# The two halves of the first q load are issued by one queue instead of two

## The chip, the core and the metric

The kernel runs on one core of a Trainium2 chip. The core has a matrix engine (TensorE, "PE" in the profile, with its weight loads as "PEld"), a vector engine (VectorE, "DVE"), a scalar engine (ScalarE, "ACT"), a general engine (GpSimd, "POOL") and a synchronisation engine (SyncE, "SP") that in this kernel does nothing but issue DMAs. DMAs are issued by SP, ACT and POOL, each into a queue of its own, and carried out by 16 DMA engines. The metric is the device time of one execution in microseconds, the median over several runs.

## What is computed

Attention over 8 batches, 12 heads, 448 positions and 64 values a head, with an RMS norm of q and k ahead of it, and behind it a dense layer with a tanh GELU and a second dense layer. Cut to what matters:

```python
q: (8, 12, 448, 64); k, v the same; g_q, g_k: (64,); moe_w_in: (768, 2048); moe_w_out: (2048, 768)

def rmsnorm(x, g):
    rms = np.sqrt(np.mean(x * x, axis=-1, keepdims=True) + 1e-06)
    return x / rms * g
q_n, k_n = rmsnorm(q, g_q), rmsnorm(k, g_k)
scores = (1 / 8) * np.matmul(q_n, k_n.transpose(0, 1, 3, 2))
attn = np.exp(scores - np.max(scores, axis=-1, keepdims=True))
attn = attn / (np.sum(attn, axis=-1, keepdims=True) + 1e-09)
x = np.matmul(attn, v)            # then to (3584, 768)
h = x @ moe_w_in
g = 0.5 * h * (1.0 + np.tanh(c * (h + 0.044715 * h * h * h)))   # c = sqrt(2 / pi)
out = g @ moe_w_out               # float32
```

## The kernel before

**Tiling.** A batch has three chunks of four heads. A chunk's q is one tile `raw` of 128 partitions by 2 x 7 x 64 floats (two heads side by side in the partitions, two more along the free side, called halves a = 0 and a = 1; seven positions to a partition), and its k another one. So a load of a chunk's q or k is 448 KB, and half a of it 224 KB. A unit (line 324) is one seventh of a chunk's keys against all queries: four matmuls into a PSUM tile and one exponential of 128 x 896 on ACT (line 337, `ex`). A batch is 21 units. Behind the units come the sums over keys and the products with v (line 384), their reciprocals and transposes on DVE, then the first dense layer (lines 422 and 473) with GELU, and the second dense layer (line 443), whose matmuls fill the gaps of the next batch's attention.

**Order.** The order on each engine is written by hand: what the program says first runs first on its engine. Each engine runs its own list in that order and waits by semaphores for what it needs. Tiles come from pools; a tile of a pool that is all in use waits until its old content has been read.

**The start**, which the change touches, is lines 613 to 723, before the first units:

- Line 614 makes the first q tile and the two loads of its halves; lines 616 to 623 add the loads of the first k in two pieces: positions 0 to 3 of each partition (`t_first`, 256 KB) and 4 to 6 (`t_rest`, 192 KB). Lines 624 and 625 issue all four. Half 0 of q is issued by SP, half 1 by ACT, both pieces of k by SP. `load` (line 115) issues part i on `engs[i]`.
- Line 626 loads the row g_k on ACT's queue (`load_g`, two pieces of 128 bytes, which land in a tile that POOL clears first, line 83); g_q came before on POOL's queue (line 91). Line 627 loads ACT's table for exponential and logarithm.
- Lines 628 and 629 issue, on SP, q and k of chunk 1 and of chunk 2 (448 KB each); lines 725 to 727 do the same for batch 1 beside the first units.
- Lines 678 to 682: ACT squares half 0 and half 1 of q (line 159), DVE sums each over 64 values (line 170); then the same for k's first piece. Lines 687 and 688 make the reciprocal roots on ACT (logarithm at line 195, exponentials at 202 and 214). Lines 690 to 692 scale q on POOL and DVE and k's first piece on DVE (line 273).
- Lines 694 to 696: POOL squares chunk 1's q and k (line 161, into a free part of the tile `g`), one square for q and two for the halves of k. DVE sums these at lines 721 to 723, behind its scaling of k's second piece at line 720. Then POOL goes on to v's loads (lines 697 and 698), chunk 2's squares (699 and 700) and the loads of the first weights (701).
- Lines 702 to 719: transposes of q and k by PE, copies to `qT` and `kT` by ACT and DVE (line 291, lines 300 to 304), and the bound `shift` for the exponentials.
- Then the units run (line 768). In the list of what goes between units, chunk 1's reciprocal roots (`rsqrt(0, 1)`) stand on ACT behind the third unit's exponential (line 734), and chunk 1's scaling on DVE behind them.

The few lines around the change:

```python
t_first, t_rest = slice(0, 4), slice(4, NT)
halves = load(0, 0, "q", 2, (nc.sync, nc.scalar))      # line 614
raws["k", 0, 0] = rawqk.tile([P, 2, NT, D], F32, tag="rawk", name="rawk")
halves += [lambda ts=ts: nc.sync.dma_start(...) for ts in (t_first, t_rest)]
for go in halves:
    go()
load_g(1, g_k, nc.scalar)
nc.scalar.preload_act_table_set(EXP_SET)
loads(0, 1)
loads(0, 2)
```

Of the kernel before, what the change touches and what calls it, by code (L numbers as in the profile page):

```python
# [17 lines left out]
def kernel(  # L18
# [11 lines left out]
    nc = tc.nc  # L30
# [84 lines left out]
    def load(b, c, n, parts=1, engs=(nc.sync,)):  # L115
        t = rawqk.tile([P, 2, NT, D], F32, tag=f"raw{n}", name=f"raw{n}")
        src = {"q": q, "k": k}[n]
        raws[n, b, c] = t
        m = 2 // parts
        return [  # L120
            lambda i=i: engs[i].dma_start(
                t[:, i * m:(i + 1) * m].rearrange("p a t d -> p a (t d)"),
                src[b, 4 * c + 2 * i * m:4 * c + 2 * (i + 1) * m].rearrange(
                    "(a r) (p t) d -> (r p) a (t d)", r=2, t=NT
                ),
            )
            for i in range(parts)
        ]
# [482 lines left out]


    t_first, t_rest = slice(0, 4), slice(4, NT)
    halves = load(0, 0, "q", 2, (nc.sync, nc.scalar))
    raws["k", 0, 0] = rawqk.tile([P, 2, NT, D], F32, tag="rawk", name="rawk")
    halves += [
        lambda ts=ts: nc.sync.dma_start(  # L617
# [278 lines left out]
```

## Time and profile before

| what | value |
|---|---|
| time, median of 3 runs | 405.6 us (405.19 to 406.0) |
| time of the profiled execution | 405.4 us |
| its span, first to last instruction | 403.6 us |
| TensorE clock that was granted | 0.999 |
| PE busy | 393.4 us, 97% of the span |
| ACT busy | 281.0 us, 70% |
| DVE busy | 257.7 us, 64% |
| POOL busy | 123.0 us, 30% |
| PE idle from the span's start to 10 us | 2.97 us |
| PE idle from 10 to 20 us | 2.59 us |
| PE idle from 20 to 30 us | 0.92 us |
| PE idle from 30 to 300 us | 0.0 us |

All times inside the profile are microseconds from the span's start. A line of the timeline has start, duration, engine, line of the program, operation, output<-inputs, shapes, count, and in brackets how long the engine sat idle before it and what ended that. A q behind an engine's name (SPq, ACTq) is its issuing part: a line with it is the issue of a DMA, not its transfer. The chain of waits is followed back from the last instruction, at each step to what released it; a DMA in it counts from its issue to its landing. A DMA lands when all the engines that carry it have reported.

### The profile page before, as it was taken

The page shows a single profiled execution, that of the slowest core. Times are in us where ns is not written, and L with a number is a line of the kernel's source. Part 1 is how long each engine was busy: PE and PEld are TensorE (multiplying, and loading weights), DVE is VectorE, ACT ScalarE, POOL GpSimd, SP SyncE. Part 2 cuts the span into 40 slices and gives each one's busy share as a digit, 9 for nine tenths or more (in the row PEclk, how much of TensorE's full clock was granted, in tenths as well). Part 3 has the DMA queues.
Part 4 walks back from the last instruction along what each step waited for, and adds up shares of the span by engine and source line. Part 5 has one row for each costly group of instructions (what it writes and reads, how often), then busy time and mean ns, then how long its engine had stood idle before and what let it go on. Part 6 is the DMA issues. An engine that isn't in the chain of part 4 may idle for free.

```text
span 403.6 us, 8096 instructions
## 1 busy us (share of the span) xinstructions
PE 393.4 (97%) x3321; PEld 209.8 (52%) x3321; DVE 257.7 (64%) x436; ACT 281.0 (70%) x382; POOL 123.0 (30%) x103
## 2 busy tenths in 40 slices
PE   7799999999999999999999999999999999999996
PEld 3365555555555555554555555555555545555564
DVE  5998858985796369845699357963698405990010
ACT  6995498868974887847975689748878359744301
POOL 4993407364007230093004540072301800000000
PEclk9999999999999999999999999999999999999999
DMA  8999995998515954169612938139413511110033
GB/s 280 312 212 208 200 211 210 239 233 228 97 41 105 256 97 143 41 162 288 107 41 63 255 60 221 40 85 275 69 41 80 115 24 39 50 47 24 2 78 80
DMA packets 65561, 54.07 MB, mean 134 GB/s; under 512 B 37364, under 2 KB 60532, under 8 KB 65524
## 3 DMA queue, kind: packets, MB, share of 16 engines
q1 hardware_dynamic: 53184, 41.48, 38.3%
q0 software_dynamic: 12112, 11.80, 18.8%
q8 instruction: 26, 0.43, 0.4%
q10 hardware_dynamic: 228, 0.28, 0.3%
q14 instruction: 11, 0.09, 0.1%
HBM read 45.61 MB, written 11.01 MB: 140 GB/s over the span
## 4 chain that ended last, share of the span: by engine, by line
PE 94%; ACT 2%; DMA 2%; POOL 1%; DVE 0%; SPq 0%; issue 0%
PE o L443 38%; PE h L422 24%; PE t L473 12%; PE t L333 9%; PE t L384 8%; ACT ex L337 2%; DMA rawq<-in_q_dram 2%; PE o L384 1%; POOL g L161 1%; PE tp L291 1%; SPq L617 0%; PE os L384 0%; DVE st L393 0%; DVE ss L170 0%; PE o L266 0%
## 5 line engine op out<-in xcount | busy, mean ns | idle before, releaser
L337 ACT ACTIVATE ex<-t,shift 128x896 bf16<-128x896 f32 x168 | 157.6, 1005 | 22.0 <-PE t L333 19.4
L443 PE MATMUL o<-wout,g 128*128 128x384 bf16 (+1 forms) x912 | 156.8, 324 | 0.0
L443 PEld LDWEIGHTS <-g 128*128 128x128 bf16 x912 | 83.6, 98 | 67.7 <-issue 18.8
L422 PE MATMUL h<-xT,win 128*128 128x448 bf16 x516 | 99.1, 352 | 0.0
L170 DVE TENSOR_REDUCE ss<-sq 128x14 f32<-128x896 f32 (+3 forms) x45 | 44.3, 999 | 49.1 <-ACT sq L159 46.1
L422 PEld LDWEIGHTS <-win 128*128 128x128 bf16 x516 | 50.5, 98 | 47.1
L428 ACT ACTIVATE g<-h 128x448 bf16<-128x448 f32 x86 | 46.6, 543 | 28.2 <-PE h L422 23.1
L453 DVE COPY osb<-o 128x384 f32<-128x384 f32 x41 | 22.7, 554 | 52.6 <-PE o L443 50.6
L333 PE MATMUL t<-qT,kT 64*64 64x448 bf16 x672 | 47.0, 359 | 3.0 <-DVE kT L300 1.0
L473 PE MATMUL t<-xT,win 128*128 128x448 bf16 x252 | 49.6, 352 | 0.0
L478 ACT ACTIVATE g<-t 128x896 bf16<-128x896 f32 x21 | 18.4, 915 | 33.0 <-PE t L473 33.0
L666 POOL COPY mark<-es 1x1 bf16<-1x1 bf16 x6 | 1.1, 177 | 131.5 <-DVE es L355 131.5
L273 POOL TENSOR_TENSOR nrmq<-rawq,rinv 128x896 bf16<-128x896 f32 (+1 forms) x21 | 34.8, 1658 | 12.0 <-DVE o L236 7.7
L473 PEld LDWEIGHTS <-win 128*128 128x128 bf16 x252 | 24.5, 98 | 22.8 <-issue 0.6
L273 POOL TENSOR_TENSOR nrmk<-rawk,rinv 128x896 bf16<-128x896 f32 x20 | 33.5, 1679 | 0.0
L333 PEld LDWEIGHTS <-kT 64*64 64x64 bf16 x672 | 17.4, 105 | 28.1 <-issue 20.8
L384 PE MATMUL t<-ex,vb 64*64 64x448 bf16 x588 | 31.6, 350 | 0.0
L451 ACT COPY osb<-o 128x384 f32<-128x384 f32 (+1 forms) x16 | 7.3, 458 | 31.5 <-PE o L443 31.5
L400 DVE STREAM_TRANSPOSE rb<-rc 128x896 f32<-128x896 f32 x24 | 26.7, 1111 | 0.8
L358 DVE TENSOR_TENSOR e<-ex 128x896 bf16<-128x896 bf16 x33 | 20.0, 607 | 9.7 <-ACT ex L337 9.4
L384 PEld LDWEIGHTS <-vb 64*64 64x64 bf16 x672 | 20.4, 107 | 11.1 <-issue 2.4
L393 DVE STREAM_TRANSPOSE st<-t 128x448 f32<-128x448 f32 x42 | 24.6, 625 | 1.0 <-PE t L384 0.9
(93 smaller groups left out, 294.5 us busy)
## 6 DMA issues: line engine op xcount, KB each, us to landing
out_dram<-osb SPq DMA_DIRECT2D x54, 192.0 KB, 2.7
rawq<-in_q_dram SPq DMA_DIRECT2D x23, 448.0 KB, 4.3
rawk<-in_k_dram SPq DMA_DIRECT2D x23, 448.0 KB, 5.5
vb<-in_v_dram POOLq DMA_DIRECT2D x7, 672.0 KB, 6.7
win<-in_moe_w_in_dram POOLq DMA_DIRECT2D x8, 384.0 KB, 11.0
wout<-in_moe_w_out_dram POOLq DMA_DIRECT2D x2, 1536.0 KB, 24.0
vb<-in_v_dram POOLq DMA_DIRECT2D x1, 448.0 KB, 10.5
qT<-nrmq SPq DMA_TRANSPOSE x19, 4.9
```

The costliest lines, as they stand in the source:

```text
L170: nc.vector.reduce_sum(sss[b][:, seat(b, c), "qk".index(n), hs, ts], squares(b, c, n, hs, ts), axis=AX.X)
L273: eng.tensor_mul(nrms[n, b, c][:, ts].rearrange("p t a d -> p a t d"), raws[n, b, c][:, :, ts], root[:, :, ts].to_broadcast([P, 2, m, D]),)
L333: nc.tensor.matmul(sc[r * R:(r + 1) * R, a, :S], kT[rs, c, t, r], qT[b][rs, c, :, r], start=True, stop=True,)
L337: nc.scalar.activation(ex[:, t], sc[:, :, :S], AF.Exp, scale=scale, bias=shift)
L384: nc.tensor.matmul(o[r][a * D:(a + 1) * D], vb[b % 2][rs, 2 * c + a, i] if what else ones[rs], es[i][rs, a], start=(i == 0), stop=(i == n ...
L393: nc.vector.transpose(st[:, r].rearrange("p a b -> p (a b)"), oas[0][r])
L400: nc.vector.transpose(rb.rearrange("p r s -> p (r s)"), rc.to_broadcast([128, 2 * S // 32, 32]))
L422: nc.tensor.matmul(h[:, :S], win[:, c, f * 128:(f + 1) * 128], xT[b][:, c], start=(c == 0), stop=(c == HP - 1),)
L428: nc.scalar.activation(g[:, f, (b % 2) * S:(b % 2 + 1) * S], h[:, :S], AF.Gelu_apprx_tanh)
L443: nc.tensor.matmul(o, g[:, f, i * 128:(i + 1) * 128], wout[:, f, lo:hi], start=(f == 0), stop=(f == nf - 1),)
L453: nc.vector.tensor_copy(osb[:, lo:hi], o)
L473: nc.tensor.matmul(h[:, j, :S], win[:, c, f * 128:(f + 1) * 128], xT[b][:, c], start=(c == 0), stop=(c == HP - 1),)
```

## The change

The second half of the first q (half 1, 224 KB) is issued by SP, not by ACT. SP's list then begins with half 0, half 1, k's first piece, k's second piece, and goes on as before; ACT's list loses its first instruction and begins with the load of g_k. On the other engines the order of instructions is the same. Semaphores are handed out to DMAs in turn, so half 1 and g_k change theirs: SP's fifth load of 448 KB (q of batch 1's chunk 0) now waits for the landing of g_k and the sixth for half 1; before these waited for half 0 and for g_k, and the fourth for half 1, where it now waits for half 0.

```diff
     t_first, t_rest = slice(0, 4), slice(4, NT)
-    halves = load(0, 0, "q", 2, (nc.sync, nc.scalar))
+    halves = load(0, 0, "q", 2, (nc.sync, nc.sync))
     raws["k", 0, 0] = rawqk.tile([P, 2, NT, D], F32, tag="rawk", name="rawk")
```

## The prediction

> **What bounds the kernel now.** I read the page's busy times first, then busy time by stretch, then the chain of waits through the first 30 us, then the timeline and the DMA issues of the first 13 us.
>
> ```profile
> span 403.6 us, 8096 instructions
> PE 393.4 (97%) x3321; PEld 209.8 (52%) x3321; DVE 257.7 (64%) x436; ACT 281.0 (70%) x382; POOL 123.0 (30%) x103
> ```
>
> By stretch (the columns behind the length are PE, PEld, DVE, ACT and POOL busy, granted clock, DMA share, GB/s):
>
> ```profile
> 20.00:30.00 10.00, 9.08 (x174) 6.36 (x177) 8.99 (x16) 9.90 (x12) 9.98 (x10) 1.00 1.13 215
> 30.00:40.00 10.00, 10.00 (x77) 5.27 (x69) 8.59 (x17) 5.57 (x8) 3.67 (x3) 1.00 1.19 208
> ```
>
> PE has its last gap near 29 us and is full from there on, so the program ends when the first attention releases PE, plus a fixed amount of matmul work. A shift of the time at which that happens goes to the end one to one; nothing else of this change does. The chain of waits says what sets it (start, duration, what):
>
> ```profile
> 2.20 6.35 DMA rawq<-in_q_dram
> 8.55 0.07 issue
> 8.62 3.47 POOL g L161 x3
> 12.09 0.02 issue
> 12.12 0.63 DVE ss L170
> 12.75 0.02 issue
> 12.77 0.33 ACT lg L195
> ```
>
> It does not pass through the halves that are moved. It passes through the load of chunk 1's q: issued at 2.20, landed at 8.55, squared by POOL with chunk 1's k until 12.09, summed, and at 12.77 in ACT's logarithm. From there to 28.9 ACT is idle for 0.15 us only. So 12.77 is the time to watch. The timeline around it:
>
> ```profile
> 4.12 1.05 ACT L159 ACTIVATE sq<-rawq 128x448 f32<-128x448 f32 x2 [0.52 <-DMA rawq<-in_q_dram]
> 5.08 0.61 ACT L159 ACTIVATE sq<-rawk 128x512 f32<-128x512 f32 x1
> 8.62 1.68 POOL L161 TENSOR_TENSOR g<-rawq 128x896 f32<-128x896 f32 x1 [0.98 <-DMA rawq<-in_q_dram]
> 9.20 2.80 ACT L337 ACTIVATE ex<-t,shift 128x896 bf16<-128x896 f32 x3
> 12.77 0.32 ACT L195 ACTIVATE lg<-ss,eps 128x28 f32<-128x28 f32 x1 [0.77 <-DVE ss L170]
> ```
>
> ACT is done with the first three exponentials at 12.00 and waits 0.77 us. The path of the moved halves (squares at 4.12, first exponential at 9.20) has that slack of 0.77 us against the path that decides; POOL waited 0.98 us for chunk 1's q. The issues, and issue to landing of the first four (last column):
>
> ```profile
> 0.74 0.41 SPq L121 DMA_DIRECT2D rawq<-in_q_dram  x1
> 0.74 0.40 ACTq L121 DMA_DIRECT2D rawq<-in_q_dram  x1
> 1.19 1.10 ACTq L86 DMA_DIRECT2D grow<-in_g_k_dram  x1
> 1.22 0.94 SPq L617 DMA_DIRECT2D rawk<-in_k_dram  x2
> 2.20 0.47 SPq L121 DMA_DIRECT2D rawq<-in_q_dram  x1
> ```
>
> ```profile
> rawk<-in_k_dram SPq DMA_DIRECT2D x1, 256.0 KB, 3.5
> rawq<-in_q_dram SPq DMA_DIRECT2D x1, 224.0 KB, 3.4
> rawq<-in_q_dram ACTq DMA_DIRECT2D x1, 224.0 KB, 3.2
> rawk<-in_k_dram SPq DMA_DIRECT2D x1, 192.0 KB, 4.6
> ```
>
> Half 0 landed at 0.74 + 3.4 = 4.1, half 1 at 3.9, k's first piece at 4.7, the second at 6.3.
>
> **Issues.** SP issues one DMA more, a pitch of 1.22 - 0.74 = 0.48 us. All behind it move by that: half 1 at 1.22 (was 0.74 on ACT), k's pieces at 1.70 and 2.17, chunk 1's q at 2.68 and k at 3.19, chunk 2's q at 3.71. ACT loses its 0.40 us issue; g_k's can start when its tile is cleared (0.88) instead of 1.19, and the table load ends near 3.3 instead of 3.60. Nothing waited for that table: the squares waited for data until 4.12.
>
> **Chunk 1's q, the term on the path.** The same 1344 KB are moved up to and with it, in the same order. The DMA engines are full from 2.5 us (398 GB/s in the stretch 2.5 to 3.0, 365 in 5.5 to 6.0), so SP's later issue is covered as long as its queue doesn't run dry: half 0 alone is 224 KB, 0.59 us at 380 GB/s, and the next issue comes 0.48 us behind. What can be lost is the start: by the packet records ACT's queue moved 76 KB of the 108 KB that went before 2.5 us. Lost whole, 76 KB at 380 GB/s is 0.20 us; made up by SP's queue, nothing. I take the middle, +0.1. If the cover is gone, the price is the pitch, +0.48. Downwards, two rows bound a gain: POOL's wait of 0.98 us, and ACT's of 0.77 us plus the 0.4 us that the halves may gain (below); so no more than some 1.1 us.
> The Trainium skill (DMA: Bandwidth & Descriptors, Rules for kernel authors) says that spreading DMAs over issuing engines brings no bandwidth, as all run on the same 16 DMA engines, and saves issue time only. By that this term is 0.0 instead of +0.1.
>
> **The halves.** Half 0 no longer shares the engines: I estimate its landing 0.59 us before the pair's 4.1, at 3.5, and half 1's at 4.1 to 4.2. ACT's two squares, 0.53 us each, then run 3.5 to 4.03 and 4.2 to 4.73 instead of 4.12 to 5.17: 0.4 us gained. On the other side, if half 1 takes 3.4 us from its issue at 1.22, it lands at 4.6, just when the second square began: nothing gained. Either way it is worth 0 at the end, because it ends in the wait before 12.77.
>
> **k's first piece, the hidden risk.** In the packet records g_k's and g_q's 128-byte packets pass two of the DMA engines at 4.15 to 4.24, and k packets of 0.81, 0.90 and 0.93 us (others take 0.04 to 0.07) start at 4.25, 4.74 and 6.14. Two of the sixteen engines are then late: k's second piece is in on eleven engines by 5.3 and on the last at 6.33, chunk 1's q on fourteen by 7.31 and on the last two at 8.36 and 8.55. k's first piece was just through. Now that piece is at best as early and g_k's row up to 0.31 earlier, so the first piece can be hit. The nearest row is the second piece's lag, 6.33 - 5.22 = 1.1 us: the first piece then lands at 4.7 + 1.1 + 0.1 = 5.9. Its square starts at 5.9 instead of 5.08; 0.2 us of that is slack (the square ended at 5.69, DVE took its sum at 5.89), so the first exponential moves 0.64 us, to 9.84, and the three end at 12.64: still inside the slack. Price 0.
> The Trainium skill (same page, Specifications) puts line rate at 512 bytes and above, with a read-modify-write below; g's rows are below, and the long packets behind them agree. It changes no term of the sum.
>
> **Waits renumbered.** Batch 1's first q waits for g_k (landed 4.9) instead of half 0, up to 0.6 us later than 4.33. Four 448 KB loads are queued ahead of it then, of which the last three alone are 3.5 us at 380 GB/s: 0.
>
> **Sum.** +0.1 us: span 403.7, time 405.5 for the profiled execution's 405.4. The median shown is 0.2 above that execution, so 405.7.
>
> **Rivals.**
> 1. Slower: both rows of g hit before k's first piece is through. Then it has the whole lag that chunk 1's q had, 1.9 us at the trace's two late engines (8.55 against 6.66 for the twelfth engine), and lands at 4.7 + 1.9 + 0.1 = 6.7. The square starts 1.64 late, the first exponential 1.44 late at 10.64, the third ends at 13.44; DVE scales k's second piece until 9.74 + 1.44 = 11.18, and its three sums (1.61 + 0.62) end at 13.41. The logarithm comes at 13.44, +0.67. Should all three long packets (2.64 us) fall on one engine ahead of it, +1.4. I take 0.9: 406.5. It decides from a first exponential 0.77 late. For it: piece and rows were 0.1 us apart. Against: the rows may come before the piece's packets are there.
> 2. Faster: g_k's row, now first in ACT's queue, passes while the engines still wait for their first data (packets of 0.3 to 0.6 us near 1.9), so one stall vanishes; chunk 1's q lands at 7.5, POOL starts 1.0 us earlier, the logarithm comes at 11.77, as ACT (three exponentials done 0.4 earlier, 11.6) allows: -1.0, 404.6. Against: g_q, issued by POOL, comes at 4.17 as before.
> 3. SP's queue runs dry: +0.48, 406.1. Against: 0.59 us of data per half against 0.48 of issue.
> That the change doesn't do what it says is excluded: the order of issues shows the half on SP.
>
> **Chances.** Forecast 0.42 (own range 405.3 to 406.2), rival 1 0.34, rival 2 0.17, rival 3 0.07. About 0.2%, 0.8 us, is what a measurement can tell from no change. Rival 1 gives "slower" 0.31 of its 0.34, with 0.02 from rival 3; rival 2 is "faster" with 0.16; "same" keeps 0.51. The range reaches into both: 404.7 to 406.9.
>
> **What would show it.** Right: half 0's square starting near 3.6, ACT still idle before the logarithm, chunk 1's q landing within 0.3 us of 8.55. Rival 1: k's first piece landing past 6 and no idle time before the logarithm. Rival 2: POOL's first square of chunk 1 before 8. Wrong altogether: a gap of PE behind 29 us.

## The result, and the profile after

| | before | changed |
|---|---|---|
| median, 22 runs each | 404.64 us | 405.99 us |
| lowest and highest | 404.14, 406.28 | 404.71, 408.28 |
| span of the profiled execution | 403.6 us | 404.2 us |

The ratio is 1.0028, with a 95% interval from 1.0018 to 1.0038: in these runs the change costs 1.1 us, 0.3%; twelve more runs of it, below, gave 1.0015 (0.9998 to 1.0031), so the size is less sure than that interval says. The page of the changed kernel:

```profile
span 404.2 us, 8096 instructions
PE 395.1 (98%) x3321; PEld 210.1 (52%) x3321; DVE 257.9 (64%) x436; ACT 281.4 (70%) x382; POOL 123.1 (30%) x103
```

The busy work is nearly the same; what moved is the start. The chain of waits through the first 30 us of the changed kernel (start, duration, what):

```profile
1.22 0.41 SPq L121
1.63 0.04 issue
1.67 4.04 DMA rawk<-in_k_dram
5.71 0.02 issue
5.73 0.64 ACT sq L159
```

It now starts with SP's issues and goes through the load of k's first piece, issued at 1.67 and landed at 5.71; before, that piece was issued at 1.22 and landed at 4.7. ACT's timeline of the changed kernel (some lines left out):

```profile
3.40 1.14 ACT L159 ACTIVATE sq<-rawq 128x448 f32<-128x448 f32 x2
5.73 0.63 ACT L159 ACTIVATE sq<-rawk 128x512 f32<-128x512 f32 x1 [1.20 <-DMA rawk<-in_k_dram]
6.27 0.29 ACT L195 ACTIVATE lg<-ss,eps 128x14 f32<-128x14 f32 x1
10.09 1.01 ACT L337 ACTIVATE ex<-t,shift 128x896 bf16<-128x896 f32 x1 [0.41 <-PE t L333]
11.47 1.97 ACT L337 ACTIVATE ex<-t,shift 128x896 bf16<-128x896 f32 x2 [0.37 <-PE t L333]
13.34 0.31 ACT L195 ACTIVATE lg<-ss,eps 128x28 f32<-128x28 f32 x1
```

The halves gained what they were to gain: their squares start at 3.40 instead of 4.12. But the next instruction in ACT's list is the square of k's first piece. ACT stands for 1.20 us until that lands, and q's logarithm, which needs nothing of k, stands behind it and comes at 6.27 instead of 5.91. The first exponential moves from 9.20 to 10.09, and the logarithm of chunk 1 from 12.77 to 13.34: +0.57, against +0.6 in the span. The idle times in front of the exponentials (0.41 and 0.37, ended by PE) are a second loss; the granted clock (the number between POOL's column and the DMA share) explains them. First the kernel before, then the changed one:

```profile
8.00:9.00 1.00, 0.74 (x11) 0.39 (x8) 0.81 (x5) 0.97 (x4) 0.38 (x1) 1.00 1.04 396
```

```profile
7.00:8.00 1.00, 0.31 (x5) 0.26 (x5) 0.97 (x4) 0.85 (x3) 0.98 (x1) 0.98 1.02 323
8.00:9.00 1.00, 1.00 (x12) 0.86 (x9) 0.81 (x2) 0.83 (x3) 0.00 (x1) 0.50 1.01 330
9.00:10.00 1.00, 1.00 (x7) 0.17 (x6) 0.85 (x5) 0.65 (x3) 1.00 (x1) 0.50 1.00 367
10.00:11.00 1.00, 1.00 (x10) 0.23 (x6) 0.79 (x3) 0.91 (x1) 1.00 (x2) 0.50 1.05 403
11.00:12.00 1.00, 1.00 (x9) 0.28 (x5) 1.00 (x2) 0.63 (x2) 1.00 (x2) 0.81 1.05 403
```

TensorE runs at half clock from 7.96 to 11.38, while the first units run. PE's wait ahead of it is no longer than before (again the kernel before first):

```profile
7.18 0.19 PE L704 MATMUL t<-gbf,rows 32*128 32x32 bf16 x2 [1.88 <-DVE nrmq L273]
```

```profile
7.69 0.19 PE L704 MATMUL t<-gbf,rows 32*128 32x32 bf16 x2 [1.87 <-DVE nrmq L273]
```

Why k's first piece is late shows in the DMA rates (last column, GB/s), first the changed kernel, then the kernel before in a second profiled execution:

```profile
3.00:3.50 0.50, 0.50 (x3) 0.27 (x2) 0.00 (x0) 0.45 (x2) 0.00 (x0) 1.00 1.09 347
3.50:4.00 0.50, 0.50 (x3) 0.15 (x1) 0.00 (x0) 0.50 (x2) 0.00 (x0) 1.00 0.92 227
```

```profile
3.00:3.50 0.50, 0.50 (x3) 0.28 (x2) 0.00 (x0) 0.50 (x1) 0.00 (x0) 1.00 1.03 365
3.50:4.00 0.50, 0.50 (x3) 0.15 (x1) 0.00 (x0) 0.08 (x1) 0.00 (x0) 1.00 1.03 333
```

Where the halves end and k's first piece begins, the changed kernel moves 227 GB/s; the kernel before 333, and 364 in its first profile. By 8 us 1.75 MB are moved instead of 2.00 and 2.05.

### The profile page after: what moved, and what is told of

Read it like the earlier page. It is cut to its first block, busy times and chain, and to the rows that moved or that the text cites. A ratio compares the mean times of both kernels' runs of the same rounds, so it can differ in the third digit from the quotient of the medians.

```text
span 404.2 us, 8096 instructions
## 1 busy us (share of the span) xinstructions
PE 395.1 (98%) x3321; PEld 210.1 (52%) x3321; DVE 257.9 (64%) x436; ACT 281.4 (70%) x382; POOL 123.1 (30%) x103
## 4 chain that ended last, share of the span: by engine, by line
PE 95%; ACT 2%; DMA 1%; DVE 0%; issue 0%; SPq 0%; DVEq 0%
PE o L443 38%; PE h L422 24%; PE t L473 12%; PE t L333 10%; PE t L384 8%; ACT ex L337 2%; PE tp L291 1%; PE o L384 1%; DMA rawk<-in_k_dram 1%; PE o L266 0%; SPq L121 0%; PE os L384 0%; DVE st L393 0%; ACT sq L159 0%; DVE kT L300 0%
## 5 line engine op out<-in xcount | busy, mean ns | idle before, releaser
L443 PEld LDWEIGHTS <-g 128*128 128x128 bf16 x912 | 83.6, 98 | 67.7 <-issue 18.8
```

The source lines that it names most:

```text
L443: nc.tensor.matmul(o, g[:, f, i * 128:(i + 1) * 128], wout[:, f, lo:hi], start=(f == 0), stop=(f == nf - 1),)
```

## The experiments

Twelve kernels were run, four at a time on one chip, each beside 35 runs of the kernel before. The spread is wide: the kernel before had runs from 404.2 to 404.6 and others from 405.4 to 406 in every group, so its median differs by up to 1.0 us from one set of runs to the next (404.64, 405.65, 405.36, 405.4). Its lowest time is steady (404.14, 404.21, 404.18, 404.25), and each profile shows where its execution lost time. So I read lowest times and profiles first. (The lowest of twelve runs is a little above that of 35 by chance: twelve runs of the kernel before had 404.37.) Of the ratios below, only two lie clear of 1: q's roots first, and one load with k held. Of the 105 runs of the kernel before beside these kernels, 13 had a clock under 0.998.

| kernel | issue, landing of k's first piece | GB/s, 3.5 to 4.0 us | MB by 8 us | first exponential | chunk 1's logarithm | span | lowest, median us | runs with a clock under 0.998 |
|---|---|---|---|---|---|---|---|---|
| before, first profile | 1.22, 4.69 | 364 | 2.00 | 9.20 | 12.77 | 403.6 | 404.14, 404.64 | |
| before again | 1.22, 4.66 | 333 | 2.05 | 9.13 | 11.81 | 402.6 | 404.37, 405.1 | 1 of 12 |
| changed | 1.67, 5.71 | 227 | 1.75 | 10.09 | 13.34 | 404.2 | 404.71, 405.99 | 7 of 22 |
| changed again | 1.67, 5.12 | 228 | 1.74 | 9.12 | 12.69 | 403.5 | 405.29, 405.58 | 3 of 12 |
| 22 idle matmuls | 1.67, 5.68 | 232 | 1.70 | 9.62 | 12.73 | 403.6 | 404.92, 405.32 | 0 of 12 |
| q as one load | 1.27, 4.83 | 366 | 2.04 | 9.16 | 12.07 | 402.9 | 404.48, 404.96 | 0 of 12 |
| k's first piece by ACT | 0.75, 4.59 | 387 | 2.00 | 9.83 | 12.51 | 403.4 | 404.93, 405.61 | 4 of 12 |
| no rows of g | 1.67, 5.56 | 167 | 1.78 | 9.49 | 12.49 | 407.5 | 404.70, 405.67 | 3 of 12 |
| g_q later | 1.66, 5.39 | 306 | 1.81 | 9.32 | 12.46 | 403.3 | 404.95, 405.54 | 1 of 12 |
| q's roots first | 1.66, 5.52 | 188 | 1.73 | 10.04 | 13.67 | 404.5 | 405.02, 406.16 | 6 of 12 |
| one load, k held | 1.84, 5.71 | 133 | 1.64 | 9.71 | 13.41 | 404.5 | 405.19, 406.38 | 7 of 12 |
| before, k held | 1.84, 6.14 | 158 | 1.73 | 10.56 | 13.89 | 404.9 | 405.11, 405.79 | 1 of 12 |
| before, 22 idle | 1.21, 4.95 | 359 | 1.95 | 9.66 | 13.31 | 404.1 | 404.29, 405.31 | 0 of 12 |
| one load, 22 idle | 1.27, 5.01 | 334 | 2.03 | 9.69 | 12.37 | 403.3 | 404.46, 404.97 | 3 of 12 |

One relation holds through the table: span minus the time of chunk 1's logarithm is 390.8 to 391.1 us in all rows but one. (The exception, without g's rows, had a wait of PE for a load of weights, 2.67 us until 64.85, and half clock from 64.3 to 67.7, far from the start.) So that one time carries the result.

**The kernel before again.** No edit.

> The kernel before once more, as the measure for the others. In the profile of the changed kernel TensorE stood at half the clock from 7.96 to 11.38 us; in that of the kernel before never after 3.49. If the kernel before is only exposed to the late piece and to no clock loss, its granted clock is 0.999 to 1.000 in all runs; if its phase against the clock's 3.4 us steps is as open, some runs show 0.996 or less and are 0.5 us or more longer. Ratio to the kernel before 1.000 within 0.1% either way.

Ratio 0.9987 (0.9958 to 1.0016). One run of 12 was under 0.996. The surprise is its profile:

```profile
9.13 2.80 ACT L337 ACTIVATE ex<-t,shift 128x896 bf16<-128x896 f32 x3
11.81 0.32 ACT L195 ACTIVATE lg<-ss,eps 128x28 f32<-128x28 f32 x1
```

The logarithm follows the third exponential without a gap: chunk 1's q landed at 7.35 here, not at 8.55, and the 0.77 us of slack that the first profile showed are not there. Its chain of waits starts with half 0 of the first q, and goes on through the squares:

```profile
0.74 3.29 DMA rawq<-in_q_dram
4.03 0.02 issue
4.05 0.58 ACT sq L159
```

**22 idle matmuls, change kept.**

```diff
-    idle(16, warm())
+    idle(22, warm())
```

> Change kept; 22 instead of 16 idle matmuls ahead of the first transposes, so that TensorE's gap before them shrinks from 1.87 us to under 0.8. Theory A (k's first piece lands 1 us late, ACT's squares are in order, the slack of 0.77 us is used up): the loss stays, +0.8 to +1.3 us against the kernel before, k's first piece still lands past 5.4. Theory B (the longer gap costs one step of the clock at half speed): granted clock 0.999 or more in every run and the loss is gone, within 0.3 us of the kernel before. Theory C (SP's longer list of issues delays chunk 1's q by its 0.48 us): the loss stays, +0.5.

The clock was 0.998 or more in all 12 runs, and the lowest time still 0.7 us above that of the kernel before in the same group (404.21); ratio 0.9987 (0.9961 to 1.0013). The late piece stays (5.68). So the clock is a part, not the whole.

**All of the first q as one load.**

```diff
-    halves = load(0, 0, "q", 2, (nc.sync, nc.sync))
+    halves = load(0, 0, "q")
```

> Change kept in that all of the first q comes by SP's queue ahead of k, but as one load of 448 KB: one issue, so k's pieces and chunk 1's q are issued at 1.22, 1.69 and 2.20 as in the kernel before. C: the loss is gone, within 0.3 us of the kernel before. A: the bytes ahead of k's first piece are those of the changed kernel and so is its landing, past 5.3: the loss stays, +0.8 to +1.3 us, or is larger by up to 0.3 as the first square waits for both halves (near 3.9 instead of 3.4). B: as A, with clocks below 0.997 in some runs.

The same bytes in the same queue, one issue fewer: k's first piece is issued at 1.27, lands at 4.83, no dip, ratio 0.9975 (0.9947 to 1.0003). The order of the bytes is not what costs; C's prediction held, A's did not.

**k's first piece by ACT, both halves by SP.**

```diff
-        lambda ts=ts: nc.sync.dma_start(
+        lambda ts=ts, eng=eng: eng.dma_start(
...
-        for ts in (t_first, t_rest)
+        for ts, eng in ((t_first, nc.scalar), (t_rest, nc.sync))
```

> Change kept; k's first piece is issued by ACT ahead of g_k's row, beside the two halves of q on SP, and chunk 1's q is then issued at 2.2 as before. A: the piece runs beside the halves, lands by 4.7, its square no longer stops ACT for more than 0.3 us, and the time is within 0.3 us of the kernel before, or faster by up to 0.4 if half 0 still lands at 3.5. B: TensorE's gap shrinks below 1.9 us and the clock stays 0.999. C: gone as well, as SP's list is again as long as before.

The rates are full and the piece is early (4.59), but half 1 now shares the engines with it and lands at 1.21 + 4.04 = 5.25; the first exponential comes at 9.83. Ratio 0.9986 (0.9958 to 1.0014), lowest 404.93: all theories had missed that the bytes put ahead of half 1 cost as much.

**The changed kernel again.** No edit.

> The changed kernel once more, on the chip of the three others. So far: k's first piece landed at 5.71 and 5.68 in the two profiles with this order, at 4.69 and 4.66 in those of the kernel before, and the first exponential came at 9.6 to 10.1 instead of 9.1 to 9.2. Expected: again past 5.3, first exponential at 9.5 or later, +0.7 to +1.4 us against the kernel before; clock of 0.996 or less in about a third of the runs (7 of 22 so far), and these longer by some 0.5 us.

Ratio 1.0015 (0.9998 to 1.0031), lowest 405.29. The dip is there (228 GB/s), the piece less late (5.12), its first exponential no later than before; here chunk 1's q, landed at 8.38, set the logarithm (12.69). The low rates reach both chains; which one is hit harder differs between executions. For chunk 1's q this is not shown by its landing: the kernel before, without a dip, had 8.55 in its first profile.

**No rows of g.**

```diff
-    load_g(0, g_q, nc.gpsimd)
+    for j in range(2):
+        nc.gpsimd.memset(grow[j * 32:j * 32 + 1], 1.0)
...
-    load_g(1, g_k, nc.scalar)
```

> The rows g_q and g_k aren't loaded; POOL writes ones in their place, so the gain is left out of the computation. Otherwise the changed kernel. Theory A1 (g_q's 128-byte packets, now at 3.4 to 3.6 in the middle of k's first piece, stall two DMA engines by one packet of some 0.85 us each): no k packet of more than 0.5 us near 3.8, k's first piece lands by 4.95, the first exponential comes at 9.2 or before, within 0.3 us of the kernel before or faster. Theory A2 (SP's later issue alone makes the piece late, g's rows have nothing to do with it): it still lands past 5.3, loss stays at +0.7 or more.

This kernel leaves the gain out. Theory A1 falls: without g's rows the piece lands at 5.56, the dip is 167 GB/s. Ratio 1.0016 (0.9992 to 1.0039).

**g_q later.** The issue stands behind the identity in POOL's list.

```diff
-    load_g(0, g_q, nc.gpsimd)
     ident = consts.tile([128, 128], BF16)
     make_identity(nc, ident)
+    load_g(0, g_q, nc.gpsimd)
```

> POOL issues g_q's row behind the making of the identity, some 1.3 us later (2.6 instead of 1.29); otherwise the changed kernel. A1: g_q's packets pass after k's first piece is through (4.6 or later), which lands by 4.95; first exponential near 9.2; the loss is gone to within 0.3 us, unless g_q's own landing (near 5.4) holds POOL's part of q by more than 0.2 us. A2: the piece still lands past 5.3 and the loss stays at +0.7 or more.

Inconclusive: the issue came at 1.49, 0.2 us later and not 1.3, and landed at 4.2, as in the changed kernel (4.1). Piece at 5.39; ratio 1.0010 (0.9994 to 1.0025).

**q's roots ahead of k's square.**

```diff
-    square(0, 0, "k", nc.scalar, ts=t_first)
-    total(0, 0, "k", ts=t_first)
     nc.vector.transpose(gcols, gprod)
...
     rsqrt(0, 0, q_only, (0,), slice(0, NT), twice=True)
+    square(0, 0, "k", nc.scalar, ts=t_first)
+    normed(0, 0, "q", nc.gpsimd, t_first)
+    normed(0, 0, "q", nc.vector, t_rest)
+    total(0, 0, "k", ts=t_first)
     rsqrt(0, 0, k_only, (1,), t_first)
     square(0, 0, "k", nc.scalar, ts=t_rest)
-    normed(0, 0, "q", nc.gpsimd, t_first)
-    normed(0, 0, "q", nc.vector, t_rest)
```

> q's roots and its scaling are put ahead of the square and the sum of k's first piece on ACT and DVE; loads as in the changed kernel. The late piece then no longer holds q. B (TensorE's gap ahead of q's transposes costs clock): transposes of q start near 6.5 instead of 7.7, the granted clock is 0.998 or more in all runs, 0.3 to 0.6 us better than the changed kernel on average. A (the late piece holds its own chain to the first unit): the first exponential stays at 9.4 or later as kT's first part comes from the late piece, and +0.3 us or more against the kernel before remain.

A held (first exponential 10.04); B's number failed. q's transposes did start at 6.6, but PE then waited 1.04 us for k, and 6 of 12 runs were under 0.998. The gap had only been moved. Ratio 1.0026 (1.0007 to 1.0045).

**k's first piece held back, in both orders of q.** SP waits for a marker in k's tile behind seven small fills on DVE; in one kernel with q as one load, in the other with the halves of the kernel before.

```diff
+    for _ in range(7):
+        nc.vector.memset(rows[:, :D], 0.0)
+    nc.vector.memset(raws["k", 0, 0][:1, 0, 0, :1], 0.0)
     halves += [
```

> All of the first q as one load on SP, as in the run with one issue fewer (which had no loss: k's first piece landed at 4.83, 2.04 MB were moved by 8 us, 366 GB/s between 3.5 and 4.0). Only SP's issue of k's first piece is held back, by a marker that DVE writes into its tile behind seven small fills, from 1.27 to about 1.7, the time it has in the changed kernel (1.67). Theory D (the time of that issue decides: the two halves are through at 3.4 and the queue runs dry before k's first packets are there): the rate between 3.5 and 4.0 falls under 300 GB/s, k's first piece lands at 5.0 or later, at most 1.9 MB are moved by 8 us, the loss of the changed kernel is back, +0.5 us or more against the kernel before. Theory E (it is the boundary between two halves in one queue, or one queue alone, whatever the issue time): no dip, the piece lands by 4.9, within 0.3 us of the kernel before.

> The kernel before, halves side by side by two queues, with the same hold on the issue of k's first piece (about 1.7 instead of 1.22). D: the halves are through at about 3.4 all the same, so the dip, the late piece (5.0 or later) and the loss (+0.5 us or more against the kernel before) appear without the change. E: nothing of that, within 0.3 us of the kernel before.

The hold came to 1.84 instead of 1.7. DMA rates, first with q as one load, then with the halves side by side in two queues:

```profile
3.50:4.00 0.50, 0.50 (x3) 0.15 (x1) 0.00 (x0) 0.00 (x0) 0.00 (x0) 1.00 0.55 133
4.00:4.50 0.50, 0.50 (x3) 0.18 (x2) 0.00 (x0) 0.48 (x1) 0.17 (x1) 1.00 0.69 198
```

```profile
3.50:4.00 0.50, 0.50 (x3) 0.15 (x1) 0.00 (x0) 0.28 (x2) 0.00 (x0) 1.00 0.79 158
4.00:4.50 0.50, 0.50 (x3) 0.18 (x2) 0.07 (x1) 0.50 (x2) 0.00 (x0) 1.00 0.43 119
```

D held in both: engines busy for 0.43 to 0.79 of the time where they were full, the piece at 5.71 and 6.14, lowest times 0.9 us above 404.25. Ratios 1.0019 (1.0003 to 1.0036) and 1.0011 (0.9993 to 1.0028); the second alone would not be clear of no change. A late issue makes the dip with one queue or two, with or without a boundary between halves. Whether it is the issue of k's first piece or that of the loads behind it, the runs don't tell: these move with it (k's second piece is issued by 1.76 in all kernels without a dip and from 2.15 in all with one).

**22 idle matmuls in the kernel before, and in the one with one load.**

> The kernel before with 22 instead of 16 idle matmuls. B: no run below a granted clock of 0.998 (of the kernel before, 7 of 35 and 3 of 35 runs were, at 407 to 410 us); the lowest time and the lower quartile as for the kernel before (404.2 and 404.4), the upper part of the distribution nearer: -0.2 to -0.6 us in the mean. If the clock is no part of it: the same spread as the kernel before.

> One load of 448 KB for the first q on SP, and 22 idle matmuls: the version that might beat both. D and B: k's first piece lands by 4.9, clock 0.998 or more in all runs; the lowest time 404.3 to 404.6, and the mean at or under that of the kernel before by up to 0.5 us. If the two queues are worth more than SP's issue: +0.3 us or more.

Neither beats the kernel before: ratios 1.0001 (0.9985 to 1.0017) and 1.0013 (0.9987 to 1.0040). In both profiles the clock rose only at 6.2, the idle matmuls ran at half speed until then and held q's transposes to 7.7: the extra ones cost where they were to protect. The three low clocks of the second are of 0.992, at 407.8 to 408.8 us: by the share lost (0.8% of 403 us at half clock is 6.4 us, an estimate) two steps of half clock and not one.

## Why the prediction came out as it did

The range held (404.7 to 406.9) and the direction was that of the forecast, but +0.1 us was forecast and +1.1 measured (+0.6 in the repeat, which is not clear of no change), and the number was not reached by its own steps. Of the signs that were to show it right, half 0's square came early as said (3.40); but ACT had no idle time before the logarithm, and chunk 1's q landed at 8.93, 0.38 after 8.55. In that profile DVE had chunk 1's sums at 13.11, and ACT came to them at 13.34, so k's piece and the clock set the end there, not chunk 1's q.

- **The time to watch** was right: the logarithm of chunk 1 carries the span, to 0.3 us over 13 of 14 profiles.
- **Issues** were right: pitch 0.48, k's first piece at 1.67 against 1.70 forecast; chunk 1's q came at 2.84, 0.16 later than said.
- **Chunk 1's q, the step that failed.** It said that SP's later issue is covered, 0.59 us of data per half against 0.48 us of issue. It is not covered: where the halves are through, at about 3.4, and the piece issued at 1.67 takes over, the rate falls to 227 GB/s. This is rival 3's dry queue, at its edge in the changed kernel (the engines are still marked busy for 0.92 of the time at 227 GB/s, with single packets of 0.85 us) and plain in the held kernels (0.43 to 0.79 at 119 to 198). It has a tail: the rate is 301 GB/s from 6 to 7 us, against 348. By 8 us 0.25 to 0.3 MB are missing, at 380 GB/s 0.65 to 0.8 us, where the term said 0.1 and rival 3 0.48. The landing of chunk 1's q doesn't show this by itself: it lies between 7.12 and 9.09 in the six profiles without a dip, and between 7.64 and 9.19 in the eight with one. The bytes do: 1.95 to 2.05 MB against 1.64 to 1.81. That the issue time is the cause, the one load (no dip) and the two held kernels (dip) show from both sides. How it acts is not shown. The first packets are not late: by the packet records the first of k's piece starts at 3.15 to 3.40 in every profile, whether it was issued at 0.75 or at 1.84. It is those behind them: half of its 256 packets have started by 3.69 to 3.88 without a dip, and by 3.93 to 4.38 with one.
- **The halves** gained 0.72 us at their squares (3.40 for 4.12; forecast 0.6). Worth nothing at the end, as said, though for another reason: k's square stands in ACT's list ahead of q's logarithm.
- **k's first piece** was forecast at 5.9 and landed at 5.71. The size was right by luck, for the cause was wrong (and the repeat had 5.12): the rows of g, on which rival 1 rested too, aren't needed for it (without them 5.56). Nor for the long packets: without the rows some take 0.85 and 0.93 us, and in the second profile of the kernel before none behind the rows takes over 0.54. The third long packet of the prediction, at 6.14, has the row size of a 448 KB load (1792 bytes), not of k's pieces.
- **Price 0 for a late piece** was wrong because the slack was that of one execution. The profile before was of a run at 405.4, with chunk 1's q in at 8.55 and 0.77 us of slack. In the other profile of the same kernel, of a run at 404.42, half 0 of q is the start of the chain and there is no slack. The median of 404.64 lies near that one (13 of the 22 runs lie under 404.8), and in such runs a late first exponential goes to the end.
- **Left out altogether: the clock.** Idle matmuls keep TensorE busy until 5.31 before and 5.82 in the changed kernel; the wait behind them is as long in both (1.88 and 1.87). By the trace's clock records full clock began at 3.49 and at 4.55, so the same wait lies elsewhere in the clock's steps of 3.41 us: before, PE worked 1.82 us of the step from 3.49 to 6.90 and the clock stayed; in the changed kernel it worked 1.54 us of the step from 4.55 to 7.96 and the clock fell. Transposes at 7.18 instead of 7.69 would have added 0.5 us to that step, an estimate; that this would have kept the clock is not shown. In the 22 runs, six with a clock of 0.995 or 0.996 lie at 405.9 to 406.5, and the fifteen at 0.998 or more have a median of 405.44. Some 0.7 us in about a quarter of the runs is 0.2 us of the mean; the rest would be the late data. This is an estimate: no clock is on record for the 22 runs of the kernel before, which has low clocks too (13 of 105 runs, against 10 of 34 of the changed kernel).
- **The rule of the Trainium skill** that issuing from several engines saves issue time only (DMA: Bandwidth & Descriptors, Rules for kernel authors) held in its wording: rates are as full with one queue (366 GB/s) as with two (364). Reading 0.0 out of it was the mistake: the issue time was the effect.

Open: why the rates stay low until 8 us after a dip that is over by 5, how a later issue slows the packets behind the first ones, whether the long packets in the dip wait for the queue or for memory, how much work in a step keeps the clock, and why chunk 1's q lands at 7.35 in one execution of the kernel before and at 8.55 and 9.09 (22 idle) in others. No run settles it.

## What to carry to other kernels

One issue more in a queue can cost more than its own time: comparing the bytes of one load with the time of one issue (0.59 against 0.48 us) said that nothing would run dry, and the rate fell all the same. So when an issue at the start of a kernel moves, look at the DMA rate where one load takes over from the next, and at the engine that waits for loads in order: it passes the delay on to work which doesn't need them. And take slack from more than one execution: a wait of 0.77 us in one profile can be no wait in the run that makes the median.

## What was not expected of the hardware

- SP needs 0.41 us to issue 224 KB. k's first piece is spread by a late issue, not shifted: issued at 1.27 (one load) the first of its 16 engines reports at 4.43 and the last at 4.83; issued at 1.84 (one load, k held) the first at 4.53 and the last at 5.71.
- TensorE fell to half clock for one step of 3.41 us after a wait of 1.87 us, in which it had worked about 1.5 us of the step (4.55 to 7.96, idle from 5.82 to 7.69). The Trainium skill (TensorE: Matmul & The Clock Gate, HAM oscillation — how this bites in real kernels) warns of gaps longer than about 3.4 us; here the shorter one was enough, and with q's roots first two waits of 0.40 and 1.04 us were (the step from 5.30 to 8.71). But the kernel before kept full clock through a wait of 1.88 us. PE's work in a step doesn't sort these either: after 1.54 and 1.92 us of work the clock fell, after 1.82 it stayed. That the steps run free of the kernel, as the same page says (Part 1: The HAM clock gate), agrees with the clock records: full clock came at 3.49, 4.55 and 6.31 us in three profiles with the same 16 idle matmuls.
